# Retention by pairs of sequences: one visit takes the same chunk of two, and the head of the kernel is written anew

## The chip, the cores and the metric

The kernel runs on one core of a Trainium2 chip, as one program. The metric is the device time of the whole program in microseconds; a number is the median of several runs. The engines are named as the profile names them: PE (matmuls), PEld (PE's weight loads), DVE, ACT and POOL (elementwise work), SP (issues nearly all DMAs).

## The reference

Three parts run one after the other; only the last result is an output.

```
q, k, v: (4 sequences, 8 heads, 576 tokens, 64), fp32
ret = (q @ k.T / 8 * Dmat) @ v      # Dmat[i,j] = gamma_h ** (i - j) for i >= j, else 0
x   = ret as (2304 tokens, 512)
h   = x @ w_in  (512 x 2048);  g = max(h, 0) + log1p(exp(-|h|));  x2 = g @ w_out (2048 x 512)
h2  = x2 @ w2_in (512 x 2048); r = max(h2, 0);                    out = (r * r) @ w2_out
```

## The kernel before

**Retention** is computed in chunks of 64 tokens: 9 chunks in a sequence, 36 in all. A chunk's visit has two halves. `step_s(c)` multiplies k and q of the chunk to scores (`pb`, 8 matmuls of 64x64, one for each head) and adds k times v to the running state (`st`, 8 matmuls, except in a sequence's last chunk); DVE masks the scores into the chunk's tile (L368, two instructions) and ACT copies the state into the next chunk's tile (L373, two). `step_o(c)` multiplies masked scores and state with q and v (`po`, 8 matmuls), and DVE takes the result out of PSUM, times a table of decay `xw` (L399). `scale_v` (L338) multiplies a chunk's v by decay factors as soon as it is loaded. A chunk comes in two loads of 256 KB, the q/k half on the lower 64 partitions and the k/v half on the upper. Three chunk buffers (`LOADS`) turn over, so chunk c+2 is loaded in the visit that ends chunk c-1.

**First MLP** (softplus). Tokens go by five tiles of 512, 384, 512, 512 and 384; each has 16 steps, one for each 128 columns of w_in. All operands are split into a high and a low part, and three products are added. Step f computes `g1` (L451, 12 matmuls over all tokens of the tile into the PSUM tile `ph`), ACT and DVE turn ph into softplus (ACT L465, 466, 467; DVE L472, 475, 478, the last one reading ph again) and split it (gh on ACT L487, gl on DVE L488), and PE does `g2` of two steps earlier (L503, 12 matmuls into `acc`). ph takes two PSUM banks in turn (`h_bank`); the scores `pb` of a visit are written into the bank whose turn comes next (`pb_next`), and `po` into a bank of its own (`ps_at`).

**What else runs in the first MLP.** Tile 0's steps each split weights of the first MLP (`weights(j)` says how many are done by step j, 32 in all: two ACT passes L144 and L145, a DVE pass L149, then hi on ACT L177 and lo on DVE L178). Tiles 1 to 4 split the second MLP's weights in 144 small `pump_step`s, spread evenly, 2.4 for each step (`store_s` L186 to 189 and some DVE additions), and send them to DRAM. Tile t's steps also hold the visits whose tokens tile t+1 needs (`attend`): 6, 8, 8 and 6 chunks in tiles 0 to 3.

**Second MLP** (from 491 us on): a product scheme with seven instead of eight block products, on the split weights, PE after PE without gaps. `raw` and `sring` tiles of it take the room of the chunk buffers and x operands; scratch tiles s1, u2, u3 take that of the `xw` tables. Results are stored by SP (L695).

**Order.** Inside `tc.manual_schedule()` (all of the head in before) instructions stand in each engine's stream as written. Elsewhere a scheduler orders each engine's stream. Every engine works through its own stream in order. The head of before loads the first 8 chunks into buffers of their own, runs them one after the other with small matmuls in between (`keep_warm`), then steps 0 and 1 begin.

## Time and profile before

| | us |
|---|---|
| median of 3 runs (861.13 to 861.98) | 861.15 |
| profiled execution | 860.06 |
| its span in the profile | 858.3 |
| busy: PE | 837.6 (98%) |
| busy: DVE | 685.9 (80%) |
| busy: ACT | 468.1 (55%) |
| bytes moved by DMA | 185.22 MB, mean 216 GB/s |

The profile is of one execution. The busy shares are means over stages that differ, so the rows further down give them by stage; the bounds of these stages are the starts of the first product of step 0, of step 2, of tiles 1 to 4, and of the second MLP. A matmul row that says x16 for eight matmuls counts two passes of fp32 for each.

### The profile page before, as it was taken

The page shows a single profiled execution, that of the slowest core. Times are in us where ns is not written, and L with a number is a line of the kernel's source. Part 1 is how long each engine was busy: PE and PEld are TensorE (multiplying, and loading weights), DVE is VectorE, ACT ScalarE, POOL GpSimd, SP SyncE. Part 2 cuts the span into 40 slices and gives each one's busy share as a digit, 9 for nine tenths or more (in the row PEclk, how much of TensorE's full clock was granted, in tenths as well). Part 3 has the DMA queues.
Part 4 walks back from the last instruction along what each step waited for, and adds up shares of the span by engine and source line. Part 5 has one row for each costly group of instructions (what it writes and reads, how often), then busy time and mean ns, then how long its engine had stood idle before and what let it go on. Part 6 is the DMA issues. An engine that isn't in the chain of part 4 may idle for free.

```text
span 858.3 us, 16848 instructions
## 1 busy us (share of the span) xinstructions
PE 837.6 (98%) x6168; PEld 765.6 (89%) x6168; DVE 685.9 (80%) x1277; ACT 468.1 (55%) x886; POOL 9.0 (1%) x12
## 2 busy tenths in 40 slices
PE   8799999999999999999999999999999999999998
PEld 6677788989878888777899999999999999999998
DVE  4789998998799868886699788898597986686964
ACT  3589998677667754774487521355321454111453
POOL 2100000000000000000000000000000000000000
PEclk9699999999999999999999999999999999999999
DMA  8856773998288614892186277888988788887885
GB/s 205 220 170 196 209 231 108 275 265 259 49 266 282 198 25 137 268 288 69 50 257 215 69 219 247 261 279 284 293 260 249 243 260 261 287 250 251 248 262 167
DMA packets 117781, 185.22 MB, mean 216 GB/s; under 512 B 10562, under 2 KB 64450, under 8 KB 117698
## 3 DMA queue, kind: packets, MB, share of 16 engines
q1 hardware_dynamic: 117700, 184.16, 70.4%
q8 instruction: 49, 0.80, 0.4%
q14 instruction: 32, 0.26, 0.1%
HBM read 145.32 MB, written 38.80 MB: 215 GB/s over the span
## 4 chain that ended last, share of the span: by engine, by line
PE 68%; DVE 11%; ACT 9%; DMA 8%; issue 2%; SPq 1%; POOL 0%; ACTq 0%; DVEq 0%
PE acc L503 12%; PE ph L451 12%; PE py L678 9%; PE py L613 9%; PE px L678 6%; PE pz L678 6%; PE px L613 6%; PE pz L613 6%; DMA wo_raw<-in_moe_w_out_dram 2%; DVE e L478 2%; DVE ct L187 2%; DMA s2d<-ct 1%; DVE l L475 1%; DMA wi_raw<-in_moe_w_in_dram 1%; DMA ch<-in_kv_dram 1%
## 5 line engine op out<-in xcount | busy, mean ns | idle before, releaser
L451 PE MATMUL ph<-xh,wi 128*128 128x512 f32 (+1 forms) x640 | 146.1, 370 | 1.9 <-DVE e L478 1.5
L451 PEld LDWEIGHTS ph<-xh,wi 128*128 128x128 f32 x640 | 116.3, 188 | 19.7 <-DVE e L478 2.9
L503 PE MATMUL acc<-gh,woh 128*128 128x512 f32 (+1 forms) x320 | 121.1, 380 | 0.7 <-ACT gh L487 0.7
L503 PE MATMUL acc<-gh,wol 128*128 128x512 f32 (+1 forms) x320 | 118.7, 371 | 0.0
L503 PE MATMUL acc<-gl,woh 128*128 128x512 f32 (+1 forms) x320 | 118.6, 371 | 0.0
L613 PE MATMUL py<-t,sring 128*128 128x384 f32 x432 | 88.2, 338 | 0.0
L487 ACT CAST gh<-e 128x512 fp32r<-128x512 f32 (+1 forms) x80 | 45.9, 573 | 62.5 <-DVE e L478 56.7
L451 PE MATMUL ph<-xl,wi 128*128 128x512 f32 (+1 forms) x320 | 79.0, 368 | 0.3 <-DVE xl L422 0.3
L613 PEld LDWEIGHTS py<-t,sring 128*128 128x128 f32 x432 | 75.3, 188 | 2.1 <-DVE uring L791 0.7
L472 DVE SCALAR_TENSOR_TENSOR e<-e 128x512 f32<-128x512 f32 (+1 forms) x80 | 50.9, 637 | 24.3 <-ACT l L467 23.2
L488 DVE TENSOR_TENSOR gl<-e,gh 128x512 fp32r<-128x512 f32 (+1 forms) x80 | 50.9, 636 | 23.7 <-ACT gh L487 23.1
L503 PEld LDWEIGHTS acc<-gh,woh 128*128 128x128 f32 x320 | 60.3, 189 | 9.4 <-ACT gh L487 0.8
L653 ACT CAST gh<-g 128x384 fp32r<-128x384 f32 x84 | 43.0, 513 | 46.8 <-PE px L678 16.7
L503 PEld LDWEIGHTS acc<-gh,wol 128*128 128x128 f32 x320 | 60.6, 189 | 7.8
L503 PEld LDWEIGHTS acc<-gl,woh 128*128 128x128 f32 x320 | 60.5, 189 | 7.2 <-DVE gl L488 0.2
L653 ACT CAST gring<-g 128x384 fp32r<-128x384 f32 x84 | 43.2, 514 | 42.7 <-PE py L678 18.2
L451 PEld LDWEIGHTS ph<-xl,wi 128*128 128x128 f32 x320 | 58.7, 188 | 8.3 <-DVE xl L422 0.8
L639 DVE TENSOR_TENSOR gring<-g,gring 128x384 fp32r<-128x384 f32 x84 | 46.7, 556 | 18.4 <-ACT gring L653 16.4
L639 DVE TENSOR_TENSOR gl<-g,gh 128x384 fp32r<-128x384 f32 x84 | 46.3, 556 | 18.7 <-ACT gh L653 18.4
L465 ACT ACTIVATE e<-ph 128x512 f32<-128x512 f32 (+1 forms) x80 | 44.1, 551 | 29.3 <-PE ph L451 28.9
L787 ACT COPY uring<-px 128x384 f32<-128x384 f32 x24 | 11.5, 479 | 87.7 <-PE px L613 87.7
L613 PE MATMUL pz<-t,sring 128*128 128x384 f32 x288 | 58.6, 335 | 0.0
(97 smaller groups left out, 1689.5 us busy)
## 6 DMA issues: line engine op xcount, KB each, us to landing
sring<-s2d SPq DMA_DIRECT2D x168, 256.0 KB, 3.2
sring<-o2d SPq DMA_DIRECT2D x168, 256.0 KB, 3.5
wi_raw<-in_moe_w_in_dram SPq DMA_DIRECT2D x32, 512.0 KB, 4.7
wo_raw<-in_moe_w_out_dram SPq DMA_DIRECT2D x32, 512.0 KB, 4.6
s2d<-ct SPq DMA_DIRECT2D x48, 256.0 KB, 3.4
o2d<-ct SPq DMA_DIRECT2D x48, 256.0 KB, 3.0
ch<-in_qk_t_dram SPq DMA_DIRECT2D x36, 256.0 KB, 5.1
ch<-in_kv_dram SPq DMA_DIRECT2D x36, 256.0 KB, 5.1
```

What stands on the lines that cost most here:

```text
L187: nc.vector.tensor_tensor(out=l, in0=src, in1=h, op=ALU.subtract)
L451: nc.tensor.matmul(ph[:, :n], lhsT=a, rhs=x, start=(j == 0), stop=(j == len(todo) - 1))
L465: nc.scalar.activation(out=e, in_=ph[:, :n], func=AF.Abs)
L472: nc.vector.scalar_tensor_tensor(out=e, in0=e, scalar=-2.0, in1=e, op0=ALU.add, op1=ALU.mult)
L478: nc.vector.scalar_tensor_tensor(out=e, in0=hps.pop(key)[:, :n], scalar=0.0, in1=l, op0=ALU.max, op1=ALU.add)
L487: nc.scalar.copy(h[:, :n], g)
L488: nc.vector.tensor_tensor(out=l[:, :n], in0=g, in1=h[:, :n], op=ALU.subtract)
L503: nc.tensor.matmul(acc[j][:, :n], lhsT=a, rhs=x, start=(begin and m == 0), stop=(end and m == 2))
L613: nc.tensor.matmul(ps, lhsT=a, rhs=x, start=(first and m == 0), stop=(m == len(todo) - 1), skip_group_check=True,)
L639: nc.vector.tensor_tensor(out=out, in0=a, in1=b, op=ALU.subtract)
L653: nc.scalar.copy(h, src)
L678: nc.tensor.matmul(blocks[m], lhsT=a, rhs=x, start=(first and p == n == 0 and m in opens), stop=(p == NP - 1 and n == 2), skip_group_check ...
```

## The change

- A visit takes the same chunk of two sequences, (0, 1) and then (2, 3): 18 pairs. A pair's tile holds both (`[P, 2, 3, H, CN]`), its loads are 512 KB each, and two pair buffers take the place of three chunk buffers. Masks, evictions, state copies and scale_v are instructions of twice the width; the matmuls are the same in number and size. `place` gives a pair's places in q, k, v and in the output.
- A visit runs `step_s(c)` first and `step_o(c-1)` after it. The scores use the bank of their own (`ps_at`, now full), and po goes into ph's shared bank (`in_next`). State copies come after that. Tiles 0 to 3 hold 4, 4, 4 and 3 visits.
- The decay table is made for each visit (`make_xw`, one DVE instruction into `xw_now`) in place of nine kept tables; the second MLP's scratch tiles move into a raw buffer.
- The head loads weights among the pairs, splits three weights there, loads constants on ACT's queue, and runs outside of the manual schedule from the first pair on. g1 of steps 0 and 1 is done in two halves of 256 tokens (24 more matmuls); the first half needs only pairs 0 and 1.
- Tile 0 has 5 + 2j weights split by step j. The 144 pump steps go 24, 42, 42 and 36 to tiles 1 to 4, where 38.4, 38.4, 38.4 and 28.8 went.
- Each output store is two of 64 partitions, one issued by SP and one by ACT.

```diff
-LOADS = 3
+LOADS = 2
...
+    def place(c, s):
+        return (c // SCH * 2 + s) * SCH + c % SCH
...
+    def load_part(c, half):
+        at_c = slice(place(c, 0), place(c, 1) + 1, SCH)
+        src, i = ((qk_t, 0), (kv, 1))[half]
+        nc.sync.dma_start(
+            out=chunk[c][(LO, HI)[half], :, i:i + 2],
+            in_=src[at_c].rearrange("s p i h c -> p s i h c"),
+        )
...
+    def masked(c, pb):
         for of, i in ((HI, 0), (LO, 1)):
             nc.vector.tensor_tensor(
-                out=qp[HI, i * HH:(i + 1) * HH], in0=pb[of], in1=mask[of], op=ALU.mult
+                out=chunk[c][HI, :, 0, i * HH:(i + 1) * HH],
+                in0=pb[of].rearrange("p (s h) c -> p s h c", s=2),
+                in1=mask[of].rearrange("p (s h) c -> p s h c", s=2), op=ALU.mult,
             )
...
+    def next_state(c):
+        if c % SCH < SCH - 1:
             for of, i in ((LO, 0), (HI, 1)):
-                nc.scalar.copy(chunk[c + 1][LO, 2, i * HH:(i + 1) * HH], st[of])
+                nc.scalar.copy(
+                    chunk[c + 1][LO, :, 2, i * HH:(i + 1) * HH], state[0][of]
+                )
...
+            xw = xw_now
+            make_xw(xw, c % SCH)
...
-    def g1(key, f, n):
-        ph = h_bank("ph")
+    def g1(key, f, n, begin=0):
+        if begin == 0:
+            hps[key] = h_bank("ph")
+        ph = hps[key]
...
+            for queue, half, q in ((nc.sync, LO, 0), (nc.scalar, HI, 1)):
+                r0 = place(c, q) * CN
+                queue.dma_start(
...
+        pump_load(1)
         load_chunk(0)
+        pump_load(2)
+        load_chunk(1)
+        pump_load(3)
+        load_chunk(2)
+        load_chunk(3)
...
+    pump(1)
+    early_s(2)
+    scale_v(2, nc.gpsimd)
+    early_o(2)
+    for j in range(EARLY_G1):
+        g1(j, j, P * 2)
+    early_st(2)
+    early_s(3)
...
                 c = tick[0]
-                step_o(c - 1, ps_at)
+                if c < NPR:
+                    step_s(c, ps_at.tile([P, H, CN], F32, tag="at", name="pb"))
+                if c - 1 in chunk:
+                    step_o(c - 1, in_next("po"))
                 load_chunk(c - 1 + LOADS)
                 if c < NPR:
-                    step_s(c, pb_next())
+                    next_state(c)
                 scale_v(c - 1 + LOADS)
...
-        first = (2, 2, 2, 3)[:j + 1]
-        return min(n_one, 2 + int(sum(first) + 1.9 * (j + 1 - len(first))))
+        return min(n_one, 5 + 2 * j)
...
-        g1(j, f, n)
+        g1(j, f, n, 2 * P if j < EARLY_G1 else 0)
...
-            total, i = 18 * NP, (b - 1) * KF + f
-            while n_steps[0] < min(total, -(-total * (i + 1) // (KF * last_b - 4))):
+            total, done = 18 * NP, (0, 24, 66, 108, 150)
+            goal = done[b - 1] + (done[b] - done[b - 1]) * (f + 1) // KF
+            while n_steps[0] < min(total, goal):
```

How the streams stand is shown at three places. The first is PE at the end of the head. In before (ch_518 is chunk 8, ph_500, ph_592 and ph_636 are steps 0, 1 and 2):

```order
L357 MATMUL pb_489<-ch_144 64x64 x8
L386 MATMUL po_552<-ch_144 64x64
L451 MATMUL ph_500<-xh_226,wi0_457 128x512 x8
L451 MATMUL ph_500<-xl_228,wi0_457 128x512 x4
L386 MATMUL po_552<-ch_144 64x64 x7
L357 MATMUL pb_566<-ch_518 64x64 x8
L363 MATMUL st_567<-ch_518 64x64 x8
L386 MATMUL po_676<-ch_518 64x64 x4
L451 MATMUL ph_592<-xh_226,wi0_457 128x512 x8
L451 MATMUL ph_592<-xl_228,wi0_457 128x512 x4
L451 MATMUL ph_636<-xh_226,wi0_457 128x512 x8
```

In after, first from the end of pair 1 on (ch_122, ch_127, ch_130 are pairs 1, 2, 3; ph_356 and ph_369 are steps 0 and 1; a g1 row of 256 columns is a half):

```order
L423 MATMUL po_264<-ch_122 64x64 x16
L376 MATMUL st_220<-ch_122 64x64 x16
L493 MATMUL ph_356<-xh_216,wi0_171 128x256 x8
L493 MATMUL ph_356<-xl_217,wi0_171 128x256 x4
L364 MATMUL pb_314<-ch_127 64x64 x16
L493 MATMUL ph_369<-xh_216,wi0_171 128x256 x8
L493 MATMUL ph_369<-xl_217,wi0_171 128x256 x4
L423 MATMUL po_335<-ch_127 64x64 x16
L376 MATMUL st_220<-ch_127 64x64 x16
L364 MATMUL pb_400<-ch_130 64x64 x16
L423 MATMUL po_424<-ch_130 64x64 x16
```

The first halves of steps 0 and 1 have moved in among pairs 1 and 2. Then, still PE in after, from the second half of step 1 to step 2 (ph_600), with pair 4 (ch_133) between:

```order
L493 MATMUL ph_369<-xh_216,wi0_171 128x256 x5
L364 MATMUL pb_515<-ch_133 64x64 x16
L493 MATMUL ph_369<-xh_216,wi0_171 128x256 x3
L493 MATMUL ph_369<-xl_217,wi0_171 128x256 x4
L376 MATMUL st_220<-ch_133 64x64 x16
L493 MATMUL ph_600<-xh_216,wi0_171 128x512 x8
```

Step 2's g1 stands behind st of pair 4, where chunk 8's scores, states and half of its po stood ahead of step 1's.

The second place is PE at a visit in a tile with 512 columns of g1, in before (four couples of pb and st follow one another, of which the first is shown, then g2 begins):

```order
L451 MATMUL ph<-xh,wi_457 128x512 x8
L451 MATMUL ph<-xl,wi_457 128x512 x4
L386 MATMUL po<-ch 64x64 x8
L357 MATMUL pb<-ch 64x64 x2
L363 MATMUL st<-ch 64x64 x2
```

In after eight such couples follow g1, and this is the end of the last of them and what stands behind:

```order
L364 MATMUL pb<-ch 64x64 x2
L376 MATMUL st<-ch 64x64 x2
L423 MATMUL po<-ch 64x64 x16
L545 MATMUL acc<-gh,woh_583 128x384
L545 MATMUL acc<-gl,woh_583 128x384
```

po has moved from ahead of pb and st to behind them, and there are twice as many of each.

The third place is DVE at a visit of tile 1, in before:

```order
L488 TENSOR_TENSOR gl<-e,gh 128x384
L399 TENSOR_TENSOR xr<-po,cst 128x256
L368 TENSOR_TENSOR ch<-pb,cst 64x256 x2
L472 SCALAR_TENSOR_TENSOR e<-e 128x384
L187 TENSOR_TENSOR ct<-ct 128x512
L475 SCALAR_TENSOR_TENSOR l<-e,l 128x384
L149 SCALAR_TENSOR_TENSOR ct<-wi_raw 128x512
```

And in after:

```order
L514 SCALAR_TENSOR_TENSOR e<-e 128x384
L383 TENSOR_TENSOR ch<-pb,cst 64x2x256 x2
L436 TENSOR_TENSOR xr<-po,xw_now 128x512
L517 SCALAR_TENSOR_TENSOR l<-e,l 128x384
L214 TENSOR_TENSOR ct<-ct 128x256
L520 SCALAR_TENSOR_TENSOR e<-ph,l 128x384
L189 TENSOR_TENSOR ct<-ct 128x512
L898 SCALAR_TENSOR_TENSOR xw_now<-cst 128x256
```

The eviction of po (L436, L399 in before) has moved behind the masks, each of the three is twice as wide, and make_xw (L898) is new.

## Rows read from the trace of the kernel before

**Rows 1.** Stages: window, us, busy (xcount) PE PEld DVE ACT POOL, PEclk, DMA share, GB/s

```profile
0.00:39.80 39.80, 31.49 (x466) 26.48 (x466) 22.29 (x49) 17.21 (x38) 8.98 (x12) 0.79 0.87 207
39.80:48.00 8.20, 7.87 (x81) 6.10 (x79) 7.05 (x12) 3.28 (x7) 0.00 (x0) 1.00 0.78 232
48.00:138.10 90.10, 89.02 (x570) 70.22 (x570) 82.81 (x138) 87.72 (x160) 0.00 (x0) 1.00 0.67 198
138.10:222.30 84.20, 82.19 (x754) 77.49 (x752) 72.73 (x147) 59.49 (x120) 0.00 (x0) 0.98 0.73 214
222.30:322.20 99.90, 98.92 (x752) 80.65 (x753) 84.29 (x155) 66.37 (x120) 0.00 (x0) 1.00 0.56 175
322.20:421.90 99.70, 96.02 (x626) 77.54 (x625) 75.65 (x134) 61.99 (x109) 0.00 (x0) 1.00 0.53 164
421.90:491.00 69.10, 68.24 (x383) 66.39 (x382) 60.07 (x110) 45.85 (x90) 0.00 (x0) 1.00 0.59 183
491.00:858.30 367.30, 363.86 (x2548) 360.76 (x2546) 280.97 (x537) 126.22 (x247) 0.00 (x0) 1.00 0.81 253
```

**Rows 2.** The same table, four slices of the head

```profile
0.00:10.00 10.00, 8.95 (x68) 7.86 (x68) 0.67 (x3) 2.11 (x4) 2.28 (x6) 1.00 0.71 167
10.00:20.00 10.00, 7.17 (x194) 5.89 (x194) 7.25 (x18) 4.01 (x11) 3.35 (x4) 1.00 1.05 241
20.00:30.00 10.00, 8.22 (x119) 6.40 (x114) 6.14 (x14) 4.70 (x12) 2.17 (x2) 0.50 0.94 229
30.00:40.00 10.00, 7.35 (x95) 6.50 (x96) 8.41 (x17) 6.40 (x13) 1.18 (x1) 0.64 0.79 193
```

**Rows 3.** Timeline of POOL in the head: start, us, instruction [idle before <-releaser]

```profile
31.54 1.18 POOL L338 TENSOR_TENSOR ch<-ch,cst 64x512 f32<-64x512 f32 x1 [6.50 <-DMA ch<-in_kv_dram]
```

**Rows 4.** Timeline of PE, a step with a visit and one without

```profile
322.21 1.98 PE L451 MATMUL ph<-xh,wi 128*128 128x512 f32 x8
...
325.02 0.69 PE L386 MATMUL po<-ch 128*64 128x64 f32 x16
...
325.63 0.27 PE L357 MATMUL pb<-ch 64*64 64x64 f32 x2
...
325.74 0.22 PE L357 MATMUL pb<-ch 64*64 64x64 f32 x2
...
326.09 0.22 PE L357 MATMUL pb<-ch 64*64 64x64 f32 x2
...
326.26 0.50 PE L503 MATMUL acc<-gh,woh 128*128 128x512 f32 x1
...
329.13 1.98 PE L451 MATMUL ph<-xh,wi 128*128 128x512 f32 x8
...
334.57 1.98 PE L451 MATMUL ph<-xh,wi 128*128 128x512 f32 x8
```

**Rows 5.** PE's waits, 39.8 to 491: total us, times, longest us

```profile
PE pb L357 <- DVE e L478: 5.8, 8, 1.5
PE ph L451 <- DVE e L478: 1.5, 2, 0.8
```

**Rows 6.** Instructions by line, 138.1 to 421.9: count | busy us, mean ns | idle before

```profile
L187 DVE TENSOR_TENSOR ct<-ct 128x512 fp32r<-128x512 f32 x39 | 26.8, 686 | 4.1 <-ACT ct L186 4.0
...
L465 ACT ACTIVATE e<-ph 128x512 f32<-128x512 f32 x32 | 19.0, 594 | 12.0 <-PE ph L451 11.9
...
L368 DVE TENSOR_TENSOR ch<-pb,cst 64x256 f32<-64x256 f32 x42 | 17.8, 423 | 1.3 <-PE st L363 0.6
...
L338 DVE TENSOR_TENSOR ch<-ch,cst 64x512 f32<-64x512 f32 x19 | 13.1, 690 | 1.5 <-DMA ch<-in_kv_dram 1.1
...
L373 ACT COPY ch<-st 64x256 f32<-64x256 f32 x36 | 13.0, 360 | 0.3
...
L399 DVE TENSOR_TENSOR xr<-po,cst 128x256 f32<-128x256 f32 x22 | 9.2, 419 | 1.6 <-PE po L386 1.6
```

**Rows 7.** Timeline of SP at the end

```profile
854.66 1.30 SPq L695 DMA_DIRECT2D out_dram<-xo  x3
```

More of the change, by code (lines that the diff above doesn't have):

```diff
@@ L330, in load_chunk @@
-    def load_chunk(c):
-        load_qk(c)
-        load_kv(c)
+            chunk[c] = pool.tile([P, 2, 3, H, CN], F32, tag="ch", name="ch")
+    def load_part(c, half):
[5 more added lines that the diff above has]
+        )
+    def load_chunk(c, order=(0, 1)):
+        if c < NPR:
+            if c not in chunk:
+                new_chunk(c)
+            for half in order:
+                load_part(c, half)
@@ new lines, in states @@
+    def states(c, s, h):
+        if c % SCH == SCH - 1:
+            return
+        if c % SCH == s == h == 0:
+            state[:] = [ps_st.tile([P, 2, HH, D], F32, tag="st", name="st")]
+        kk, sv = (chunk[c][:, :, i] for i in range(1, 3))
+        for to, hh in ((LO, h), (HI, h + HH)):
+            nc.tensor.matmul(
+                state[0][to, s, h, :], lhsT=kk[HI, s, hh, :], rhs=sv[HI, s, hh, :],
+                start=c % SCH == s == h == 0, stop=True, skip_group_check=True,
+            )
@@ new lines, with step_s, in_acc @@
+    each = [(s, h) for s in range(2) for h in range(HH)]
+    def step_s(c, pb):
+        for s, h in each:
+            scores(c, pb, s, h)
+            states(c, s, h)
+        masked(c, pb)
+    def next_state(c):
+        if c % SCH < SCH - 1:
+            for of, i in ((LO, 0), (HI, 1)):
+                nc.scalar.copy(
+                    chunk[c + 1][LO, :, 2, i * HH:(i + 1) * HH], state[0][of]
+                )
+    def in_acc(name):
+        return ps_acc.tile([P, H, CN], F32, tag="at", name=name)
@@ L895, with early_s, early_st @@
-        keep_warm(2)
-        step_o(last - 1, ps_acc)
-        keep_warm(6)
+        for half in (LO, HI):
+            nc.scalar.dma_start(out=cst[half, :C_XW], in_=consts[CN:P, :C_XW])
+        nc.scalar.preload_act_table_set("natural_log_exp_and_others")
+        def early_s(c):
+            pb = in_acc("pb")
+            for s, h in each:
+                scores(c, pb, s, h)
+            masked(c, pb)
+        def early_st(c):
+            for s, h in each:
+                states(c, s, h)
+            next_state(c)
@@ new lines, in early_o, with tables @@
+        def early_o(c):
+            kept = chunk[c]
+            step_o(c, in_acc("po"))
+            chunk[c] = kept
+        def tables():
+            row = rows_in.rearrange("p (m a b) -> p m a b", a=KD, b=CN)
+            spread(
+                xw_first.rearrange("p (a b) -> p a b", a=KD),
+                row[:, 0], (KD, CN), nc.scalar.copy,
+            )
+            spread(times, row[:, 1:, :, 0], (SCN - 1, KD), nc.scalar.copy)
+            for c in range(1, last):
+                make_xw(xw_soon[:, c - 1], c)
@@ new lines @@
+        pump_load(1)
+        load_chunk(0)
+        pump_load(2)
[3 more added lines that the diff above has]
+        load_chunk(3)
+        new_chunk(last)
+        new_chunk(last + 1)
+        keep_warm(14)
+        tables()
+        keep_warm(6)
+    pump(1)
+    early_s(0)
+    scale_v(0, nc.gpsimd)
+    early_o(0)
+    early_st(0)
+    keep_warm(4)
+    early_s(1)
+    scale_v(1, nc.gpsimd)
+    early_o(1)
+    early_st(1)
+    keep_warm(3)
+    pump(1)
+    early_s(2)
@@ L898 @@
+    scale_v(2, nc.gpsimd)
[4 more added lines that the diff above has]
+    early_s(3)
+    keep_warm(4)
+    scale_v(3)
+    early_o(3)
+    load_chunk(last)
+    early_st(3)
+    for c in range(last):
+        chunk.pop(c)
+    pump(1)
+    scale_v(last, nc.gpsimd)
     first.__exit__(None, None, None)
     late_wts.append(ctx.enter_context(tc.tile_pool(name="late", bufs=1, reuse_waits="tile")))
-    step_s(last, pb_acc())
-    tick[0] = last + 1
+    tick[0] = last
```

187 lines of the change are left out of this document (74 added, 113 removed).

## The prediction, made before the changed kernel was run

> **What bounds the kernel now.** I read the stage table first [rows 1]. Its stages are the head (0 to 39.8 us, until the first product of step 0), steps 0 and 1 (to 48.0), the rest of tile 0 (to 138.1), tiles 1 to 3 (to 421.9), tile 4 (to 491.0) and the second phase. From 39.8 us on, PE is busy 97% or more of nearly every stage. The second phase holds 363.86 us of PE work in 367.30 us, and the change leaves its products alone, so at most its 3.4 us of gaps are there. What can go is therefore the head, PE's own work at the visits, and PE's small stalls in the first phase. Two other engines stand close behind PE: ACT with 87.72 of 90.10 us in tile 0, and DVE with 60.07 of 69.10 in tile 4 and 84.29 of 99.90 in tile 2.
>
> In the head PE is no bound. By slices [rows 2] the DMA engines are busy for a share of 1.05 and 0.94 in 10 to 30 us, moving 241 and 229 GB/s, and TensorE's granted clock is 0.50 in 20 to 30 us, its lower level of 1.2 GHz, and 0.64 in the slice after, between its two levels. POOL waited 6.50 us for the last chunk's kv half [rows 3]. So the head is a race of loads, and the first products run when the data of 8 chunks has passed through retention.
>
> Next the timeline of one step with a visit and one without [rows 4]. Between the starts of its g1 and the next one's, the first takes 329.13 - 322.21 = 6.92 us, the second 334.57 - 329.13 = 5.44. A visit costs PE **1.48 us**: po from 325.02 to 325.63 (0.61), pb and st from 325.63 until g2 begins at 326.26 (0.63), and the rest in changes of shape (g2's first matmul takes 0.50).
>
> Last the list of PE's waits [rows 5]. Of 39.8 to 491 us, pb waits 5.8 us (8 times, at most 1.5) and ph 1.5 us (twice), all for DVE's L478. pb shares two banks of PSUM with ph, so a visit's first scores can't be written until DVE has read the bank's last ph.
>
> **The change, term by term.**
>
> *Head.* By order and size, the loads up to pair 4 are 5 weights and 10 half pairs of 512 KB, 7.86 MB. The head of before moved 1.67 + 2.41 + 2.29 = 6.37 MB in its first 30 us [rows 2]. The 1.49 MB left take 6.5 us at 229 GB/s and 7.7 us at 193, so pair 4 lands at 36.5 to 37.7. POOL scales it in 2 x 1.18 us [rows 3], st of pair 4 (0.5 us) follows at about 40, and PE, which is in order, then starts step 2's g1 at about **41**. Before it starts at 48.0 [rows 1]. Steps 0 and 1 are by then done except for their second products. Their four token halves cost no more columns, and 24 more matmuls are issued; the first two halves run under the loading of pairs 2 and 3. That is 7.0 us; I take **-6.5**, since ACT has to pass wo0, one weight more and both steps' softplus before pair 4's state copies, which it did not have to do there before. Bounds: ACT is full in tile 0, and in the new order it has about one weight (three instructions) and step 1's softplus (three) done earlier, 6 x 0.594 = 3.6 us [rows 6]. Were ACT what sets tile 0's end, the stage itself would shrink too, to -10. The other end is 0: the halves at the half clock and ACT's queue take back all of it.
>
> *Visits.* In tiles 1 to 3 there are 22 visits of one chunk before, 11 of a pair after. A pair has twice the products: po 16 instead of 8, and 16 couples of pb and st instead of 8. A couple's pitch is 0.058 us [rows 4] (325.74 to 326.09 is 0.35 for six of them); po's is 0.61 / 8 at most, of which I take 0.06 as pitch and the rest as an edge. So a pair adds 0.47 + 0.48 = 0.95 to the 1.48, and 2.43 stand against 2 x 1.48 = 2.96. That is -0.53 per pair, and 11 x 0.53 = **-5.8**. Bounds: 0, if the edges double with the work, and -6. Tile 0's visits are counted at nothing, since ACT covers them.
>
> *Stalls.* pb moves to a bank of its own, so the 5.8 us of [rows 5] lose their cause. The new order puts po where pb was: it takes ph's shared bank, but stands behind pb and st, about 1.0 us later. A wait of at most 1.5 us is mostly outlasted by that. The pumps of weight splits are also spread differently: 24 instead of 38.4 in tile 1. A split item of nine steps is two orderings and three stores of 512 columns at 0.686 and five instructions of 256 columns at 0.42 on DVE [rows 6], 5.5 us or 0.61 us a step, so tile 1's DVE loses 14.4 x 0.61 = 8.8 us of its 72.73 [rows 1]. What is late next is the next ph, which needs DVE's eviction of po from that bank. Of 5.8 + 1.5 us I take **-3.5**, between -6 and +4 (the waits come back at the eviction, as in the slower rival at part strength).
>
> *DVE and ACT at a visit.* Two old visits cost DVE 4 x 0.423 (masks) + 2 x 0.419 (eviction) + 2 x 0.690 (L338) = 3.91 us [rows 6]. A pair costs two masks and an eviction of 512 columns (0.69 each, from L338's row), one scale of 1024 (1.22, by the slope from 0.42 at 256 to 0.69 at 512) and a new make_xw of 256 (0.42), 3.71. ACT's copies are 4 x 0.360 = 1.44 before, 2 x 0.594 = 1.19 after. So total work hardly moves, and it costs nothing while the engines have idle time; what moves is its lump.
>
> *Loads.* Three chunk buffers become two pair buffers. The load of pair c+1 goes to SP in the visit that runs po of pair c-1, and waits there for that po; SP's later weight loads and stores stand behind it, as they do behind the chunk loads of before. The lead falls from two chunks to one pair, but the next visit is some four steps of 5.44 us away, and the DMA engines are busy for a share of 0.53 to 0.73 in these tiles [rows 1]. I count it at nothing. Were the cover gone, scale_v on DVE would wait for the load with softplus work queued behind it, and the price is that of the slower rival.
>
> *Tile 4.* The pump leaves it 36 steps instead of 28.8: 7.2 x 0.61 = 4.4 us more DVE work on 60.07 of 69.10 [rows 1]. The idle time of 9.0 us covers it on average, but t, the second phase's operand, is built there in long DVE instructions. I take **+2**, between 0 and +4.4.
>
> *Second phase and end.* The raw tiles and the three scratch products change their place, not their work. At the end of before, three stores take SP 1.30 us to issue [rows 7]. After, each is two of 64 partitions, on SP and ACT's queue, three issues on each queue as before: **+0.3**, between -0.2 and +1.8 (three more issues of 0.43 one after the other, and 0.5 for a later landing). The Trainium skill (DMA: Bandwidth & Descriptors, Rules for kernel authors) speaks against this edit: it says not to bother with two transfers to disjoint partition halves, since both use the same 16 engines and take turns, and to use one of 128 partitions. By it the end would be at +1.3 or so, and the sum 1 us higher; no row of before shows two queues issuing one tile, so the trace neither agrees nor disagrees.
>
> **Sum.** -6.5 - 5.8 - 3.5 + 2 + 0.3 = **-13.5 us**. The profiled execution took 860.06 us (span 858.3 and 1.8 around it), so 846.6. It lies 1.1 under the median of the runs, 861.15, so against that I forecast **847.6**.
>
> **Rivals.**
>
> *Head gain lost* (854, range 851 to 858). The first halves don't start early, since PE is in order and the loads of weights now stand ahead of pairs; or ACT's queue delays pair 4's copies; or tile 0 ends when ACT does and that is unchanged. For it: ACT's 97% in tile 0 [rows 1], and the half clock in 20 to 40 us [rows 2]. Against it: ACT is idle 22.6 of the first 39.8 us [rows 1], and the new head lets it start on whole weights there. Price: the 6.5, giving 847.6 + 6.5 = 854.1. That the change doesn't do what it says, with halves that run back to back with the rest, is this case as well.
>
> *More than forecast* (838 to 841). All of the stalls go and ACT's side gives its -10: -3.5 and -3.8 beyond the forecast, 840.3.
>
> *Slower: DVE's lump paces the visits* (about 864). Between pb and the next g1's bank, DVE must now do two masks of 0.69 and the eviction of 0.69, 2.07 us, and 2.49 if make_xw's 0.42 stands ahead; before it was one eviction of 0.42 and two masks of 0.42, 1.27. PE's cover is po (16 x 0.06, 1.0) and g2, 326.26 to 329.13 = 2.87 in a wide tile [rows 4] and 3/4 of it, 2.15, in a narrow one of 384 columns. So PE stalls once DVE reaches the masks more than about 1.8 us after pb in a wide tile, and 1.1 us in a narrow one. DVE has a backlog at a visit: pb waited for L478 at 7 or 8 of 22 visits, at most 1.5 us [rows 5]. If every pair lost 1.5 us more, 16.5 us would be gone, and 847.6 + 16.5 = 864.1 is slower than before. It decides from 1.4 us a pair on: 15.3 / 11, to reach 862.9. Against it: DVE's total work at a visit falls, tile 1's DVE is relieved by 8.8 us, and 1.5 was the longest of those waits, not their mean (5.8 / 8 = 0.7).
>
> **How the numbers follow.** The forecast (842 to 851) has 0.60, the head's gain lost 0.20 (of which 0.02 is by within 0.2% of before), more than forecast 0.08, the slower rival 0.09 (0.02 of it within 0.2%), other small mixtures near no change 0.03 (0.02 within). About 0.2% (1.7 us: 859.4 to 862.9) is what a measurement can tell from no change. So faster 0.86, same 0.06, slower 0.08. The range of 8 in 10 takes the forecast, most of the lost head and half of the larger gain: **839 to 857**.
>
> **What would show it.** Right: step 2's g1 at 40 to 42 us; tile 1 about 6 us earlier than 138.1; a step with a pair 7.8 to 8.0 us in a wide tile, against 5.44 without; no wait of pb for L520 (the old L478) in PE's waits, and less than 4 us of ph and po there together; tile 4 up to 2 us longer than 69.1; the second phase 367 to 368. Wrong: step 2's g1 after 45, or tile 1 still at 138 though step 2 came early (ACT's bound); ph or po waiting for L436 at most visits with 1 us or more (DVE's lump); a pair at 2.9 us or more of PE's time.

## The result, and the profile after

The changed kernel is slower: 865.34 us (863.21 to 867.33 in six runs) against 861.14 for the kernel before in the same session, a ratio of **1.0053 (1.003 to 1.0077)**. The forecast was 847.6. The profiled execution took 864.33 us with a span of 862.3, against 860.06 and 858.3: 4.0 us more.

The stage table of the kernel after, in the columns of [rows 1]; the head ends at 27.70 now, and steps 0 and 1 fill the second row:

```profile
0.00:27.70 27.70, 22.98 (x262) 21.00 (x262) 10.46 (x18) 9.12 (x16) 6.69 (x10) 0.75 0.95 206
27.70:52.70 25.00, 18.29 (x305) 16.70 (x305) 17.60 (x23) 14.21 (x25) 3.85 (x3) 0.86 0.81 190
52.70:144.10 91.40, 87.86 (x624) 70.87 (x625) 83.01 (x132) 85.33 (x150) 0.00 (x0) 0.98 0.66 192
144.10:225.25 81.15, 78.57 (x737) 74.81 (x736) 65.68 (x120) 50.91 (x99) 0.00 (x0) 1.00 0.59 166
225.25:327.60 102.35, 97.16 (x769) 79.25 (x769) 80.08 (x134) 64.53 (x112) 0.00 (x0) 1.00 0.65 183
327.60:424.80 97.20, 94.13 (x577) 76.76 (x577) 78.30 (x136) 63.78 (x111) 0.00 (x0) 1.00 0.58 176
424.80:491.50 66.70, 66.70 (x375) 65.11 (x375) 62.09 (x118) 48.14 (x94) 0.00 (x0) 1.00 0.69 221
491.50:862.30 370.80, 365.21 (x2556) 361.85 (x2554) 281.27 (x539) 125.72 (x248) 0.00 (x0) 1.00 0.81 251
```

Cut at the starts of the same products in both traces (for the whole table: step 2's first g1, the first g1 of each tile, the last g1 of the first phase, the last matmul), the stages compare so:

| stage, us | before | after | difference | forecast |
|---|---|---|---|---|
| to step 2's first g1 | 47.98 | 52.70 | +4.7 | -6.5 |
| rest of tile 0 | 90.11 | 91.41 | +1.3 | 0 |
| tiles 1, 2, 3 | 84.20, 99.92, 99.66 | 81.14, 102.36, 97.23 | -3.1 together | -9.3 (visits -5.8, stalls -3.5) |
| tile 4 to the last g1 | 66.83 | 64.44 | -2.4 | +2 with the next line |
| to the last matmul | 365.91 | 368.45 | +2.5 | |
| last matmul to the end | 3.68 | 4.61 | +0.9 | +0.3 |

Eight products of the second phase stand ahead of the last g1 in before, one in after. Seven at 0.17 us make 1.2 us, and that much of the two lines before the last is a shift of the cut: without it tile 4 is at -1.2 and the second phase at +1.3.

**The head.** PE's timeline, where the two first halves and the second half of step 0's g1 are the rows of 8 products of 128x256:

```profile
27.70 1.22 PE L493 MATMUL ph<-xh,wi 128*128 128x256 f32 x8 [0.37 <-ACT xh L443]
...
31.41 1.21 PE L493 MATMUL ph<-xh,wi 128*128 128x256 f32 x8
...
33.02 1.15 PE L423 MATMUL po<-ch 128*64 128x64 f32 x32
...
39.05 1.69 PE L423 MATMUL po<-ch 128*64 128x64 f32 x32 [3.04 <-ACT wi_raw L146]
...
42.93 2.07 PE L493 MATMUL ph<-xh,wi 128*128 128x256 f32 x8
...
52.70 0.47 PE L493 MATMUL ph<-xh,wi 128*128 128x512 f32 x1 [2.85 <-DVE e L520]
```

The first halves do run early, at 27.70 and 31.41. Then PE waits 3.04 us for pair 3's po. ACT is named, but DVE's timeline has the scaling of pair 3 (L353) end at 38.95, 0.1 us ahead of po; it stands behind the masks of the same pair (L383):

```profile
36.30 1.39 DVE L383 TENSOR_TENSOR ch<-pb,cst 64x512 f32<-64x512 f32 x2
37.73 1.22 DVE L353 TENSOR_TENSOR ch<-ch,cst 64x1024 f32<-64x1024 f32 x1
```

From there a chain runs to step 2: po of pair 3, its eviction, the split into xh and xl, the second halves at 42.93, step 0's softplus, and only then is one of ph's two banks free, at 52.70, after 2.85 us of waiting. Part of the chain is the clock. From 39.4 us on, behind the wait of 3.04 us, it is granted at 0.50, the level of 1.2 GHz, and again behind the wait of 2.85 us:

```profile
39.40:46.20 6.80, 6.71 (x75) 6.29 (x71) 4.93 (x5) 3.31 (x6) 2.50 (x2) 0.50 0.36 102
53.10:56.50 3.40, 3.40 (x10) 2.63 (x9) 3.28 (x6) 2.65 (x5) 0.00 (x0) 0.50 0.22 37
```

So pair 3's po takes 1.69 us against pair 2's 1.15, its states 2.33 where 1.15 is usual, and the half of step 0 takes 2.07 against 1.21: some 2.6 us together. POOL's row, as [rows 3], shows pair 4 landing at 41.28, 4 us after the forecast's 36.5 to 37.7, but its scaling is done by 43.8, nine microseconds ahead of step 2:

```profile
41.28 2.50 POOL L353 TENSOR_TENSOR ch<-ch,cst 64x512 f32<-64x512 f32 x2 [12.23 <-DMA ch<-in_kv_dram]
```

**The waits.** PE's list of 49 to 490 us, to compare with [rows 5] (total us, times, longest):

```profile
PE po L423 <- DVE e L520: 7.5, 7, 1.8
PE ph L493 <- DVE xr L436: 4.0, 6, 1.2
PE ph L493 <- DVE e L520: 3.7, 3, 2.8
PE acc L545 <- DVE gl L530: 1.2, 1, 1.2
PE ph L493 <- DVE xh L459: 0.6, 1, 0.6
```

That is 17.0 us, 14.2 without the 2.85 at step 2; the whole list of before has 9.5. pb waits no more, but po took over its place and waits longer for the same softplus instruction (L520), and a new line appears: ph waits for the eviction of po (L436). How one of the new kind arises is read from DVE's timeline at a visit of tile 1, and PE's row behind it:

```profile
205.74 0.56 DVE L514 SCALAR_TENSOR_TENSOR e<-e 128x384 f32<-128x384 f32 x1 [0.51 <-ACT l L509]
206.33 1.39 DVE L383 TENSOR_TENSOR ch<-pb,cst 64x512 f32<-64x512 f32 x2
207.75 0.69 DVE L436 TENSOR_TENSOR xr<-po,xw_now 128x512 f32<-128x512 f32 x1
```

```profile
208.50 0.44 PE L493 MATMUL ph<-xh,wi 128*128 128x384 f32 x1 [0.92 <-DVE xr L436]
```

DVE stands idle 0.51 us for ACT's logarithm of this very step, with the masks and the eviction, whose inputs are there, queued behind it; PE then waits 0.92 us for that eviction.

**The end.** SP's and ACT's queue (as [rows 7]); ACT's issue at 583.15, of a store in the middle of the second phase, and PE's only wait there, for DVE's half of a split whose cast on ACT came late behind that issue:

```profile
857.77 1.75 SPq L738 DMA_DIRECT2D out_dram<-xo  x3
857.78 2.03 ACTq L738 DMA_DIRECT2D out_dram<-xo  x3
```

```profile
583.15 1.36 ACTq L738 DMA_DIRECT2D out_dram<-xo  x2
```

```profile
587.74 0.51 PE L722 MATMUL py<-sring,gring 128*128 128x256 f32 x2 [1.29 <-DVE gring L683]
```

### The profile page after: what moved, and what is told of

It is laid out like the page before. It is cut to its first block, busy times and chain, and to the rows that moved or that the text cites. A ratio compares the mean times of both kernels' runs of the same rounds, so it can differ in the third digit from the quotient of the medians.

```text
span 862.3 us, 16741 instructions
## 1 busy us (share of the span) xinstructions
PE 830.9 (96%) x6198; PEld 766.4 (89%) x6198; DVE 678.5 (79%) x1213; ACT 461.7 (54%) x850; POOL 10.5 (1%) x12
## 4 chain that ended last, share of the span: by engine, by line
PE 63%; DVE 17%; ACT 9%; DMA 6%; issue 4%; SPq 0%; POOL 0%; DVEq 0%; ACTq 0%
PE ph L493 10%; PE acc L545 10%; PE py L657 9%; PE py L722 8%; PE pz L722 6%; PE px L657 6%; PE pz L657 6%; PE px L722 5%; DMA wo_raw<-in_moe_w_out_dram 3%; DMA wi_raw<-in_moe_w_in_dram 2%; DVE e L514 2%; DVE e L520 2%; DVE l L517 2%; ACT l L509 2%; ACT e L508 2%
## 5 line engine op out<-in xcount | busy, mean ns | idle before, releaser
L493 PE MATMUL ph<-xh,wi 128*128 128x512 f32 (+2 forms) x656 | 150.4, 371 | 8.8 <-DVE xr L436 4.0
L493 PEld LDWEIGHTS ph<-xh,wi 128*128 128x128 f32 x656 | 119.0, 191 | 29.2 <-DVE xr L436 6.8
L545 PE MATMUL acc<-gh,woh 128*128 128x512 f32 (+1 forms) x320 | 119.3, 373 | 0.0
L493 PE MATMUL ph<-xl,wi 128*128 128x512 f32 (+2 forms) x328 | 80.2, 366 | 0.7 <-DVE xl L444 0.7
L529 ACT CAST gh<-e 128x512 fp32r<-128x512 f32 (+1 forms) x80 | 45.7, 571 | 60.3 <-DVE e L520 54.3
```

The source lines that it names most:

```text
L493: nc.tensor.matmul(ph[:, begin:n], lhsT=a, rhs=x, start=(begin == j == 0), stop=(j == len(todo) - 1), skip_group_check=True,)
L529: nc.scalar.copy(h[:, :n], g)
L545: nc.tensor.matmul(acc[j][:, :n], lhsT=a, rhs=x, start=(begin and m == 0), stop=(end and m == 2))
```

## The experiments

Stages below are cut as in the table above. They come from one profiled execution each: runs that share the head of after start step 2 anywhere between 51.6 and 54.3, and those with the head of before between 46.7 and 48.5, and two traces of one kernel (h3 and g7 below) differ by 1.6 us in tile 2. So a stage's difference under about 2 us, or under 3 us at the start of step 2, decides nothing alone. Ratios are against before on the run's own chip. After was measured on one chip (1.0053), and e1 to e4, which change little, lie at 1.0086 to 1.0105 on another, so ratios of different chips that are as near as that don't order two kernels.

**Parts of the head and of the stores.** Four runs on one chip, three of them undoing or moving one thing in the head or the stores (the fourth is told with the pump):

```
e1_stores_sp     store:  (nc.scalar, HI, 1) -> (nc.sync, HI, 1)
e2_whole_g1      EARLY_G1 = 2 -> 0
e3_scale_pool    scale_v(3) -> scale_v(3, nc.gpsimd), ahead of early_s(3)
```

> After with both halves of every output store issued by SP; nothing else changes. Theory (ACT's queue): in after, ACT stands for 1.36 to 1.56 us in the issue of two stores while casts for PE wait behind it; the wait of PE for gring at 587.74 (1.57 us) and the slow start of the first unit come from it. Then the time from the last g1 to the last matmul falls from 368.45 us to about 366.5, the wait goes, and the end after the last matmul is 4.6 us plus or minus 0.5, so the run is 1.5 to 2 us under after. Rival (place of the scratch tiles in a raw buffer, or the order that the scheduler finds): the wait at gring stays, the second phase stays at 368 us, and six issues on one queue make the end 1 us longer.

> After with the g1 of steps 0 and 1 whole (12 matmuls each, no token halves); nothing else changes. Theory (pair 3 is late): in after step 0's g1 ends at 45.9 us because pair 3 has to pass loads, masks, po and split first, and step 2 waits for step 0's softplus; the halves take 1.5 us of PE each off this chain at the most. Then step 2's g1 starts 1 to 3 us later than 52.7 and the run is 0 to 3 us over after. Rival (the halves at a low clock and their place between pairs hold up the retention chain itself): pair 3's po comes earlier than 39.05 us, step 2 at 52 or earlier, the run as long as after or shorter.

> After with pair 3's scale_v on POOL ahead of its scores, where DVE does it behind the masks in after. Theory: po of pair 3 waits 3.04 us, the last 1.22 of it for this DVE instruction (37.73 to 38.95) though the data landed at 31.15; without it po starts at 37.8 instead of 39.05, and step 2 starts 1.0 to 1.3 us earlier than 52.7. Rival (the wait belongs to ACT's split of a weight or to the load of it, as the releaser named): po of pair 3 stays at 39 us, step 2 at 52.7.

e1 took 864.74 us, ratio 1.0088 (1.0053 to 1.0122). PE's wait of 1.29 us in the second phase is gone and the stretch to the last matmul is 366.63 instead of 368.45, but the end behind it grows from 4.61 to 6.29 us, as six issues stand one after the other on SP:

```profile
853.84 3.66 SPq L738 DMA_DIRECT2D out_dram<-xo  x6
```

So the second queue pays at the very end and costs before it; g6 and i2 below, with SP alone for the stores before the end, have 366.78 and 366.41 in the same stretch. e2 (1.0105, 1.0071 to 1.0138) starts step 2 at 53.34: without the early halves it lies inside the spread of the runs that have them, so they are worth little either way. e3 (1.0104, 1.0069 to 1.0139) starts it at 49.57, 3.1 us earlier. But 2.1 us of that are there at po of pair 2 already (30.92 against 33.02), ahead of the scaling that was moved, as the loads landed earlier in this execution. About 1 us is left for the edit, which is what was expected. Step 2's first eight products then stand behind a wait of 4.77 us and take 3.75 us at a granted clock of 0.50 (1.98 at 1.00); tile 0 takes 93.35 instead of 91.41, and the total doesn't move.

**The order of the loads, and what tile 0 does with it.** h1 issues four pairs' chunks ahead of the second weight and has the scaling of pair 3 on POOL:

```
 loads: c0, c1, wi0, c2, c3, wi1, wi2, c4      EARLY_G1 = 2 -> 1
+    scale_v(3, nc.gpsimd)       # ahead of early_s(3)
-    pump(1)                     # the first; the last: pump(1) -> pump(2)
```

> After with another head: the pairs' loads stand ahead of the weights' (pair 0, pair 1, one weight, pairs 2 and 3, two weights, pair 4), the weight splits stand behind the pairs they stood ahead of, pair 3's scale_v is on POOL, and only step 0's g1 is in halves. Theory (the head lost by the order of loads: in after pair 3 lands at 31.15 us and step 0's g1 ends at 45.9): pair 3 lands at about 26, step 0's g1 ends near 40, and step 2 starts at 45 to 48 instead of 52.7; the run is 4 to 8 us under after, 857 to 861. Rival (the chain of pairs through PE, DVE and ACT at a low clock sets the head, not the loads): step 2 stays at 50 us or later and the run at 863 or more.

Step 2 starts at 45.73, seven microseconds before after's; pair 3 lands at 26.75 instead of 31.15. But 861.73 us is a ratio of 1.0042 (1.0026 to 1.0059): tile 0 now takes 95.82. Its windows, whole and the first 14.3 us:

```profile
45.70:141.50 95.80, 89.36 (x624) 70.44 (x625) 85.42 (x135) 89.20 (x157) 0.00 (x0) 1.00 0.72 198
45.70:60.00 14.30, 12.82 (x95) 9.76 (x97) 11.73 (x18) 14.22 (x26) 0.00 (x0) 1.00 0.73 192
```

ACT is busy for 14.22 of the first 14.30 us: an earlier PE comes upon ACT's splits of weights. Whether ACT takes the gain back was asked in three ways. i3 and i4 move ACT's pass of L147 to POOL for the weights split in tile 0 from the fourth on, in after and in before (with before's head, and h3's pump, told below). i5 leaves that pass out, and with it the low bits of these weights; i6 leaves out the low half of the split on DVE (`lo = hi`); i7 is h1 and i5 together.

> After with ACT's second pass of the weight splits (L147, 0.75 us) on POOL for the weights of the first MLP from the fourth on: some 28 passes, 21 us, leave ACT in tile 0. Theory (ACT's work of about 108 us up to the start of tile 1, plus what it stands idle for in the head, sets this start, so PE's earlier steps buy little): tile 0 from step 2 on falls from 91.4 to 86 to 89 us, and tile 1 starts at 138 to 141 instead of 144.1. Rival (DVE or the visits set tile 0): it stays at 90.5 us or more.

> h3_before_pump (before with 24, 42, 42 and 36 pump steps) with the pass L145 on POOL as in i3_low_on_pool. Theory (ACT sets tile 0 in before too): tile 0 from step 2 on falls from 90.1 to 85 to 88 us and the run is 2 to 5 us under h3_before_pump (855). Rival: it stays at 90 and the run at 855.

> After without ACT's second pass of the weight splits (L147, 0.75 us) for the weights of the first MLP from the fourth on; DVE's pass over the words takes one operand then. This part of the computation is left out, and nothing takes its place on POOL: some 28 passes, 21 us, leave ACT in tile 0. If ACT sets tile 0: from step 2 on it falls from 91.4 to 86 to 88 us. If DVE sets it (81 of 89 us busy there): it stays at 90 or more, unless the one-operand form is faster on DVE than 0.69 us.

> After without DVE's subtraction that makes the low part of a weight (L180, 0.69 us) for the weights of the first MLP from the fourth on; the products read the high part in its place, so this part of the computation is left out. Some 28 instructions, 19 us, leave DVE in tile 0, and ACT's work is as before. If DVE sets tile 0: from step 2 on it falls from 91.4 to 86 to 88 us. If ACT sets it: it stays at 90 or more. If both stand at the limit together, each of this and i5_no_low_pass gives only a part, 1 to 3 us.

> h1_pairs_first without ACT's second pass of the weight splits (L147) for the weights of the first MLP from the fourth on; this part of the computation is left out. In h1_pairs_first step 2 starts at 45.7 us, but tile 0 takes 95.8 us from there, with ACT busy for 89.2 of them and 14.2 of the first 14.3, and PE waiting for weights (L179) and softplus. Theory (ACT takes the head's gain back once PE is early, though it is not what sets tile 0 in after, where taking the same pass away left it at 92.0): tile 0 falls to 87 to 90 us and tile 1 starts at 132 to 136. Rival (the pairs' visits, DVE or the landing of weights take it back): tile 0 stays at 94 or more.

| | step 2 starts | tile 0, us | DVE, ACT busy in it | time, ratio to before |
|---|---|---|---|---|
| after | 52.70 | 91.41 | 83.01, 85.33 | 865.34, 1.0053 |
| i5, no pass on ACT | 52.3 | 92.05 | 75.44, 70.35 | 866.04, 1.0104 (1.006 to 1.0147) |
| i6, less on DVE | 49.44 | 91.96 | 67.58, 85.93 | 863.55, 1.0062 (1.0034 to 1.009) |
| h1, pairs first | 45.73 | 95.82 | 85.42, 89.20 | 861.73, 1.0042 (1.0026 to 1.0059) |
| i7, h1 and i5 | 45.54 | 88.19 | 77.51, 74.04 | 855.08, 0.9978 (0.9954 to 1.0003) |

With the head of after, neither 15 us less on ACT nor 15 us less on DVE shortens tile 0. PE itself is busy there for 87.86 of the 91.40 us (86.34 in i5, 87.71 in i6), so no relief of another engine could have given more than about 3.5. With h1's head, leaving out the pass shortens tile 0 by 7.6 us, to 88.19 with PE busy for 86.19. So the weight splits don't set tile 0 in the changed kernel, but they stand right behind, and take back more than half of a mended head's gain. That ACT is the one of the two engines that does it is likely from its 14.22 of 14.30 us and not shown: leaving out the pass takes 15 us from ACT and, as DVE's pass then has one operand (0.42 instead of 0.69 us), 8 from DVE. i3 and i4 don't help: their ratios are 1.0103 (1.0073 to 1.0132) and 1.005 (1.0026 to 1.0075), with tile 0 at 98.4 and 95.87. In i3's tile 0 POOL does ACT's pass, DVE is busy for 90.06 us instead of 83.01 (last section), and the granted clock is 0.94 on average instead of 0.98; how much each adds isn't shown.

**The visits: which wait, and why.** h2 gives pb ph's shared bank back and po a bank of its own; h4 takes work from DVE at the visits (make_xw only in the first visit, the v scaling left out); g5 keeps the pump's steps away from a visit's step and the one before; i1 holds the step's softplus back behind the eviction:

```
h2  step_s(c, in_next("pb"));  step_o(c - 1, ps_at.tile(..., tag="at", name="po"))
h4  if c == n_first: make_xw(...);  scale_v(c - 1 + LOADS) left out
g5  free = [g for g in range(KF) if g not in visits and g + 1 not in visits]
i1  taken[0] = nc.vector.tensor_tensor(out=x, in0=po, in1=xw, op=ALU.mult)
    with tc.issue_after(taken[0].ins): softplus_b(j, n)
```

> After with the two PSUM banks of a visit exchanged back: scores in ph's shared bank, po in the bank of its own. Theory (DVE arrives late at the visits, whichever product takes the shared bank): the waits for L520 move from po to pb and grow, since pb stands 1 us earlier (7.6 us in all of tiles 0 to 3 in after, 9 to 12 now), those of ph for L436 (4.0 us) go and partly come back as waits for the masks; the run stays within 3 us of after. Rival (the new place of po in the shared bank, with its eviction ahead of the next g1, is the loss): waits of PE in tiles 0 to 3 fall by 3 us or more, and so does the run.

> After without scale_v of the pairs from the sixth on and with the decay table made only once; both are left out of the computation. It takes 1.22 + 0.42 us of DVE from each visit of tiles 0 to 3. Theory (DVE's backlog at visits makes PE wait): waits of po for L520 and of ph for L436 fall from 11.6 us to 5 to 8, tiles 0 to 3 together get 4 to 8 us shorter. Rival (the waits come from the pump steps that stand between a step's DVE instructions at the visit): they stay at 10 us or more, tiles 0 to 3 get less than 2 us shorter.

> After with the same number of pump steps in each of tiles 1 to 4, but none in a step with a visit or in the step ahead of one. Theory (PE waits at visits because pump steps of weight splits stand between a step's softplus instructions on DVE; taking scale_v and the table out did not help): waits of po for L520 and ph for L436 in tiles 1 to 3 fall from 9.5 us to 3 to 6, and these tiles together from 280.7 us to 274 to 278. Rival (ACT's part of softplus, not DVE's pump work, makes L520 late): the waits stay at 8 us or more and the tiles at 280.

> After with one order laid down on DVE: in a step with a visit, the eviction of po (and the masks, which it needs) stands ahead of this step's own softplus instructions (L514 and on). Theory (at a visit DVE stands idle for ACT's Ln of the step's own ph, while masks and eviction wait behind L514 in its stream, and the next g1 waits for the eviction): waits of ph for L436 fall from 4.0 us to under 1.5 in tiles 0 to 3, waits of po for L520 stay, and tiles 1 to 3 take 1 to 3 us less than 280.7. Rival (the eviction is late because po is, or because of earlier softplus work): L436's waits stay at 3 us or more.

h4 (1.0062, 1.0046 to 1.0078) answers the forecast's slower rival. With less work on DVE, the waits for the eviction go up, not down (PE's list, 53 to 490 us):

```profile
PE ph L494 <- DVE xr L437: 8.5, 9, 2.1
PE po L424 <- DVE e L521: 5.5, 6, 1.4
```

g5 (1.0088, 1.0059 to 1.0118) clears the same steps of the pump, and its list has 4.7 and 6.8 us in these two lines. The amount of work isn't what makes the eviction late. i1 lays down nothing but an order on DVE, and the eviction's wait nearly goes; its DVE at the same visit, and its list of 45 to 490 us:

```profile
206.18 0.56 DVE L531 TENSOR_TENSOR gl<-e,gh 128x384 fp32r<-128x384 f32 x1 [0.58 <-ACT gh L530]
206.75 1.39 DVE L383 TENSOR_TENSOR ch<-pb,cst 64x512 f32<-64x512 f32 x2
208.17 0.69 DVE L437 TENSOR_TENSOR xr<-po,xw_now 128x512 f32<-128x512 f32 x1
208.78 0.55 DVE L515 SCALAR_TENSOR_TENSOR e<-e 128x384 f32<-128x384 f32 x1
```

```profile
PE po L424 <- DVE e L521: 8.7, 6, 1.9
PE ph L494 <- DVE xr L437: 0.8, 3, 0.4
```

That settles the order as the cause of the eviction's 4.0 us. po's wait stays (8.7); why L520 is late for it, no run settles. And i1 gives tiles 1 to 3 only 1.2 us, less than the spread: 863.6, 1.0056 (1.0032 to 1.008). Its trace has two stretches there that after's doesn't have, each behind a wait of po (1.33 and 1.94 us):

```profile
186.00:190.00 4.00, 4.00 (x21) 3.93 (x16) 3.94 (x8) 3.33 (x8) 0.00 (x0) 0.57 0.90 280
364.00:368.00 4.00, 4.00 (x11) 3.15 (x11) 3.81 (x7) 2.11 (x4) 0.00 (x0) 0.57 0.93 339
```

PE is busy throughout at a granted clock of 0.57: 2 x 4 x 0.43, some 3.4 us by estimate, about what the shorter waits had given. h2 shows the same, that fewer waits need not help. Its wait of pb is back, as in [rows 5], and all waits together are 8.5 us, yet it takes 864.09 us (1.0069, 1.0041 to 1.0096). Two windows of it, and the matmuls that open the second:

```profile
269.80:275.30 5.50, 4.30 (x53) 3.36 (x51) 5.07 (x9) 4.57 (x10) 0.00 (x0) 1.00 0.59 162
275.30:283.00 7.70, 7.70 (x69) 6.64 (x70) 6.75 (x14) 5.64 (x9) 0.00 (x0) 0.56 0.96 263
```

```profile
275.28 1.92 PE L364 MATMUL pb<-ch 64*64 64x64 f32 x32 [1.20 <-DVE e L520]
```

PE was busy for 4.30 of 5.50 us, the last of its waits being the 1.20 us ahead of pb; then the granted clock is 0.56 for 7.7 us, mostly its lower level, and the 32 products of pb take 1.92 us, where 1.15 is usual. This is the slowest of h2's four runs (866.34; the others 861.02 to 865.68), so it shows how a short wait can cost, and not that it makes up h2's median.

**The pump.** e4 gives after the old even spread of the pump, h3 gives before the new one, alone; g7 is h3 again on another chip:

```
-  while n_steps[0] < min(total, -(-total * (i + 1) // (KF * last_b - 4))):
+  goal = done[b - 1] + (done[b] - done[b - 1]) * (f + 1) // KF
+  while n_steps[0] < min(total, goal):
```

> After with the pump schedule of before (2.4 steps of weight splits in each step of tiles 1 to 4, 38.4 a tile). Theory: DVE's backlog at the visits makes the waits of po for L520 and of ph for L436 (9.5 us in tiles 1 to 3), so moving 14.4 pump steps back into tile 1 brings tile 1 to 82.5 to 84 us from 81.1, with waits of 2 us or more for L520 and L436 there, and leaves tile 4 at 64.5; the run is 0 to 3 us over after. Rival (the spread is what makes tile 2 long, 102.4 against 99.9 before): tile 2 falls to 100 and the run gets 1 to 2 us shorter than after.

> Before with one part of the change alone: 24, 42, 42 and 36 pump steps in tiles 1 to 4 in place of 38.4, 38.4, 38.4 and 28.8. Theory (the relief of tile 1 is real and paid back in tiles 2 and 3): tile 1 falls from 84.2 to 81 to 82.5 us, tile 2 grows by 0 to 2.5, tiles 3 and 4 by 0 to 1; the run is within 2 us of before. Rival (it costs in tile 4, as the prediction had it): tile 4 grows by 2 us or more. The head is before's, so its steps 0 to 2 show how far the head's times differ from run to run.

> The kernel of h3_before_pump once more, with more rounds: before with 24, 42, 42 and 36 pump steps in tiles 1 to 4. If the 0.25% measured first is its own, the ratio is 0.996 to 0.999 with an interval under 1, and tile 1 is again 1 to 2 us shorter than before's 84.2; if it was chance, the interval holds 1 and goes over it.

e4 is at 1.0086 (1.0057 to 1.0114), and its tile 1 takes 82.90 us instead of 81.14. h3 is at 0.9975 (0.995 to 1.0) and g7 at 0.9963 (0.9948 to 0.9978): of the whole change, this one part is a gain by itself, some 3 us. Where it comes from is less sure. Tile 1 takes 82.52 and 82.77 in them instead of 84.20, but its granted clock is 1.00 there and 0.98 in the trace of before [rows 1], and 84.20 x 0.02 is as much. Tile 4 with 65.1 takes no more than before's 66.83, of which 1.2 is the shift of the cut.

**What mends it.** g6 takes h1's head, g5's pump and ACT's queue for the last product's stores alone; i2 is g6 with i1's order on DVE.

> The head of h1_pairs_first (pairs' loads ahead of the weights'), the pump steps of g5_pump_off_visits, and output stores on SP alone except those of the last product, which go half to ACT's queue. Theory: the three repairs add up: tile 1 starts at 141 to 142 us as in h1_pairs_first, tiles 1 to 3 take 274 to 278, from the last g1 to the last matmul 366.6 instead of 368.5, the end stays 4.6: 854 to 859 us, level with before. Rival (they hinder each other, or before's lead lies in tile 0, which none of them mends): 859 us or more, still over before by 0.2% or more.

> g6_all_mended with the order of i1_evict_first added. Theory: waits of ph for L436 fall from 5.3 us to under 2 and the run is 2 to 3 us under g6_all_mended (858.9). Rival: the waits change their name and the run stays within 1 us of it.

g6 is level with before: 858.87, 0.9997 (0.9981 to 1.0012). i2 is the fastest of all, **852.41 against 858.41, 0.9924 (0.9896 to 0.9952)**, below both kernels; its interval just overlaps that of g7 (0.9948 to 0.9978). Its tiles 1 to 3 are 79.93, 99.24 and 96.72, 7.9 us below before's. PE's timeline of a step with a pair that waits for nothing:

```profile
317.93 1.98 PE L494 MATMUL ph<-xh,wi 128*128 128x512 f32 x8
...
321.83 1.15 PE L424 MATMUL po<-ch 128*64 128x64 f32 x32
...
325.79 1.98 PE L494 MATMUL ph<-xh,wi 128*128 128x512 f32 x8
```

The step takes 325.79 - 317.93 = 7.86 us, 2.42 more than a step without a visit.

## Why the prediction was wrong, point by point

*The head, -6.5, measured +4.7.* This step failed most. It took the landing of pair 4 as what sets step 2. But step 2's g1 needs a bank of ph, both banks hold steps 0 and 1 until their second halves are done, and these need pair 3, not pair 4. The forecast counted that "four token halves cost no more columns" and didn't follow them: landing, masks, scaling, po, split, halves at the half clock (2.07 us instead of 1.21), softplus, bank. Pair 3 lands at 31.15 in after because three weights' loads stand ahead of it; the first eight chunks of before had landed by 25.97, with one weight ahead. h1, which mends that order, moves step 2 by 7 us. It also moves the weight splits behind the pairs, and pair 3's scaling to POOL; the scaling alone is worth about 1 us (e3), and the loads and the splits weren't tried apart. The landing of pair 4 itself came 4 us later than worked out.

*Tile 0, 0, measured +1.3.* The bound that "ACT is full in tile 0" was held as a possible gain. It was the opposite: PE's early start meets weight splits that aren't earlier (h1, i7). In after itself the tile's length hangs on neither ACT nor DVE alone (i5, i6). PE's own work is 87.86 us of it, and the +1.3 is inside the spread and no more than the half clock behind step 2's wait makes (3.4 us at 0.50, 1.7 by estimate). What sets the other gaps stays open.

*Visits, -5.8: right.* The forecast's price of a pair is 2.43, and i2's step shows 2.42. Over tiles 2 and 3, a step with a visit, less its waits and the 5.44 of a step without, takes 1.47 us on average in before (14 visits; 1.48 was forecast) and 2.37 in after (7).

*Stalls, -3.5, measured +4.7 of waits from step 2 on.* The wrong sign. That pb's cause would go was right, and that the bank's wait could come back at the eviction stood among the bounds (+4). Two things failed. The forecast let po, which stands 1.0 us later than pb did, mostly outlast the wait for DVE's last softplus instruction; po waited 7.5 us for it. And the order on DVE was missed: the eviction stands behind softplus instructions that themselves wait for ACT, so a bank is held for reasons that have nothing to do with its own work. The list for tiles 1 to 3 alone is 10.6 us against 6.6; with -5.8 for the visits that makes -1.8, and -3.1 was measured. Before's tile 1 at a granted clock of 0.98 (1.7 us by estimate), where after has 1.00, would fill the rest.

*Tile 4, +2, measured -1.2; second phase and end, +0.3, measured +2.2.* In tile 4 PE is busy for 66.70 of 66.70 us beside DVE's 62.09, so the pump's steps cost it nothing (h3 and g7 neither), and the +2 wasn't there. The stores cost 1.3 in the middle, where ACT issues them ahead of a cast that PE's product hangs on (e1); no term of the sum had this. At the end they cost 0.9, inside the bounds. The Trainium skill (DMA: Bandwidth & Descriptors, Rules for kernel authors) advised one transfer of 128 partitions instead of two disjoint halves. The traces agree with its direction: 3.68 us of end with whole tiles, 4.61 with halves on two queues, 6.29 with halves on one. Only the halves were tried with the pairs, so how whole tiles would do in this kernel is not shown.

*The rivals.* The head's gain was lost, but worse than to nothing. The slower rival named nearly the measured time, 864.1, and the right place, po's eviction ahead of the next g1. That its time came out near is luck: the stalls are 8.2 us off the forecast, the head 11.2. Its reason, too much work in one lump on DVE, fell with h4 and g5; for the eviction, the order of the lump was the reason (i1).

## What to carry to other kernels

When loads are moved, follow the last data that each early step needs through every engine to the buffer that the next step waits for, not only to its landing; a gain on one engine is also to be checked against the engine that stands right behind, at the place where the gain is to be used. On an in-order engine, work that frees a buffer for PE belongs ahead of work whose inputs aren't there yet: here that order turned a level kernel (g6, 0.9997) into one at 0.9924 (i2), each against before on its own chip. In after alone it took the eviction's waits away and left the total where it was (i1): with another wait beside it, the one that goes may give nothing. A change of several parts is worth splitting: one part here was a gain by itself (0.9963), and was hidden by the others.
